# Two units of a pair of heads begin together: one visit of TensorE per pair in an attention that runs inside an MLP

## The chip, the cores and the metric

One NeuronCore of one Trainium2 chip runs the whole program. The metric is the device time of one execution in microseconds, lower is better. The engines have short names here: PE is TensorE (matmuls; PEld its weight loads), ACT is ScalarE, DVE is VectorE, POOL is GpSimd, SP is SyncE, which issues nearly all DMAs.

## The reference

Windowed causal attention with a linear bias (window 128, 8 batches, 8 heads, 576 positions, 64 features per head), and then an MLP with the Mish activation on its output (4608 tokens, 512 to 2048 to 512), in float32:

```python
scores = scale * q @ k.T                      # scale = 1/8
bias = -slope[h] * |i - j|
scores = where(0 <= i - j < 128, scores + bias, -1e9)
attn = softmax(scores)
x = (attn @ v), heads side by side            # 4608 x 512
h = x @ w_in
g = h * tanh(softplus(h))                     # Mish
out = g @ w_out
```

## The kernel before, in words

**Work of the MLP.** The tokens are taken in nine groups: the first 512 positions of each of the 8 batches, and a ninth group of the 64 positions that each batch has left. For each group `c` there are two phases on PE. In the first, `first(c, j)` for j = 0..7 makes 256 of the hidden features each, into one of two PSUM tiles with the tag `s`; `mish` on ACT brings them to SBUF. In the output phase, 32 calls of `second` (8 values of j, two halves of the tokens, two tiles `t`) make the output, six matmuls of 512 columns each into `po`. A call of `second` is called an output step here, and the 32 of a group have positions 0 to 31. Both matmuls work in float32r on split operands (a rounded part and the rest), with three products for one. The split of `g` is made by `parts(c, half, j)`, four steps ahead of its use: a copy on ACT (tile `gg`, three buffers) and a subtraction on POOL.

**Work of the attention.** The attention of batch c + 1 runs inside the output phase of group c, spread between the output steps; that of batch 0 runs ahead of everything. A batch has four pairs of heads, `p` = 0..3. A pair has a first unit (`unit(b, p, 0)`, query blocks 0 and 1), a second unit (`unit(b, p, 1)`, blocks 2 and 3) and a last unit (`last_unit`, the 64 positions left, of both heads). The steps of a unit are:

- `scores`: four products on PE into a tile `s` of two PSUM banks (tag `s`, two buffers, shared with `first`). The last unit writes its scores into a free part of the first unit's tile.
- `exps(0)`, `exps(1)`: for each block and head one DVE operation (add the bias, take the minimum) and one exponential with its sum on ACT, into `pz`.
- `fold`: POOL adds the two halves of the window into one square; DVE makes reciprocals of the sums. `scale`: DVE multiplies by these.
- `weights`: four transposes on PE into the same `s` tile, then one DVE product with the two triangular masks, which spreads the square again.
- `values`: products with `v` on PE into the tile `o`, one PSUM buffer for a pair; the first unit begins it, the second ends it. `split_x` (second unit only): copy on ACT, subtraction on DVE, which give the operand `x` of the MLP.

The last unit has the same steps in small; its `fold` ends with a copy on ACT, and its `values` with a DVE copy and a DMA to `xs`.

**What sets the order.** Every engine call goes through `InOrder`, which keeps each engine's instructions in the order in which the program makes them. The order is that of a sorted list of steps, each with a time. `attention(b)` gives the steps of a batch, with one unit of time per unit of heads: unit `k = 2 p + half` starts at time k. In the output phase these times are put on the scale of output steps, `(n - 2) / 9.0 * s - 0.2` with n = 32, so that a unit of time is 3.33 output steps. Entries of `parts` stand at 2 m - 4.1 for the m-th of 16. In the output phase of group 0 four late conversions of weights (`converting`) are in the list too, at fixed positions from 0.3 to 10.1; each takes ACT, DVE and POOL.

`load_pair` and `load_v` issue the loads of the pair after next (two buffers each).

The one place where times differ between first and second unit is the end of `unit`: all units have the same list, and the products with values of unit k, at k + 1.99, come just ahead of the scores of unit k + 2.

Of the kernel before, what the change touches and what calls it, by code (L numbers as in the profile page):

```python
# [35 lines left out]
def attention_mish_mlp(  # L36
# [70 lines left out]
    def load(dst, src):  # L107
        sp.dma_start(out=dst, in_=src)

    def load_w(kind, j):  # L110

        n = 256 if kind == "i" else DM
        if kind == "i":
            src = w_in[:, j * 256 : (j + 1) * 256].rearrange("(c p) f -> p c f", p=P)
        else:
            src = w_out[j * 256 : (j + 1) * 256, :].rearrange("(c p) f -> p c f", p=P)
        if (kind, j) == last_w:

            halves = [
                xp.tile([P, 1024], U32, tag=f"x{NCC - 2 + a}", name=f"w{kind}{j}_{a}")  # L120
                for a in range(2)
            ]
        else:
            t = big(f"w{kind}{j}", U32)
            halves = [t[:, :1024], t[:, 1024:]]
            whole[(kind, j)] = t
        raw_w[(kind, j)] = halves
        for a, t in enumerate(halves):
            part = src[:, a * (512 // n) : (a + 1) * (512 // n), :]
            if bits:  # L130
                load(t.rearrange("p (c n) -> p c n", n=2 * n), part.bitcast(U32))
            else:
                load(t[:, :512].bitcast(F32).rearrange("p (c n) -> p c n", n=n), part)
# [122 lines left out]
    def load_pair(b, p):  # L256
        hs = slice(2 * p, 2 * p + 2)
        qk = at.tile([P, 2, S], F32, tag="qk", name=f"qk{b}_{p}")
        load(qk[:, 0, :], qT[b, hs].rearrange("h d s -> (h d) s"))
        load(qk[:, 1, :], kT[b, hs].rearrange("h d s -> (h d) s"))  # L260
        z = qd[p % 2]
        for i in range(2):
            r = slice(i * D, (i + 1) * D)
            load(z[r, r], qT[b, 2 * p + i, :, CH:S])
        qkv[(b, p)] = (qk, z)

    def load_v(b, p):
        cs = slice(p * P, (p + 1) * P)
        va = at.tile([P, 4, P], F32, tag="va", name=f"va{b}_{p}")
        load(va, v[b, 0:CH, cs].rearrange("(k p) d -> p k d", p=P))  # L270
        load(vb[p % 2][:64], v[b, CH:S, cs])
        qkv[("v", b, p)] = (va, vb[p % 2])
# [3 lines left out]
    def unit(b, p, half):  # L276
# [23 lines left out]
        def exps(a):  # L300
            if a == 0:
                st["mx"] = at.tile([P, 4], F32, tag="mx", name=f"mx{name}")
                st["sm"] = at.tile([P, 4], F32, tag="sm", name=f"sm{name}")
                st["pz"] = at.tile([P, 4, 256], F32, tag="pz", name=f"pz{name}")
            mx, sm, pz = st["mx"], st["sm"], st["pz"]
            n = 256 if blocks[a] else P
            for i in range(2):
                c = 2 * i + a

                dve.tensor_tensor_reduce(  # L310
                    out=pz[:, c, :n], in0=st["s"][:, i, 256 * (a + 1) - n : 256 * (a + 1)],
                    in1=nb[:, 2 * p + i, 256 - n :], scale=-SCALE, scalar=3.0e38,
                    op0=ALU.add, op1=ALU.min, accum_out=mx[:, c : c + 1],
                )
                act.activation(
                    pz[:, c, :n], pz[:, c, :n], AF.Exp, bias=mx[:, c : c + 1], scale=-1.0,
                    accum_out=sm[:, c : c + 1],
                )
# [48 lines left out]
        def split_x():  # L367
            if half == 1:
# [4 lines left out]
                    out=x[:, 1, :], in0=o, in1=x[:, 0, :].bitcast(F32), op=ALU.subtract  # L373
                )

        return [
            (0, scores), (0.02, lambda: exps(0)), (0.25, lambda: exps(1)), (0.7, fold), (0.95, scale),
            (1.3, weights), (1.99, values), (2.02, split_x),
        ]

    def last_unit(b, p):
# [61 lines left out]
    def attention(b):  # L443

        steps = []
        for k in range(2 * NP):
            p, half = divmod(k, 2)  # L450
            for u in [unit(b, p, half)] + ([last_unit(b, p)] if half == 0 else []):
                steps += [(k + d, f) for d, f in u]
            if half:
                nxt = (b, p + 2) if p + 2 < NP else (b + 1, p + 2 - NP)
                if 0 < nxt[0] < B:
                    steps.append((k + 0.03, lambda nxt=nxt: load_pair(*nxt)))
                    steps.append((k + 2.01, lambda nxt=nxt: load_v(*nxt)))
        return sorted(steps, key=lambda s: s[0])

    def last_x():  # L460
# [14 lines left out]
    def first(c, j, blocks=range(NCC)):  # L475
        if blocks[0] == 0:
            hs[j % 2] = ps.tile([P, 2, CH], F32, tag="s", name=f"h{c}_{j}", bufs=2)
        h = hs[j % 2]
        for t, cc in (
            [(t, cc) for cc in blocks for t in range(2)] if len(blocks) < NCC  # L480
            else [(t, cc) for t in range(2) for cc in blocks]
        ):
            x = xt[(c, cc)]
            for k, (w_, x_) in enumerate(((0, 0), (0, 1), (1, 0))):
                pe.matmul(
                    h[:, t, :], lhsT=w_part("i", j, w_, cc)[:, t * P : (t + 1) * P],
                    rhs=x[:, x_, :], start=(cc == 0 and k == 0), stop=(cc == NCC - 1 and k == 2),
                )
# [3 lines left out]
    def mish(c, j):  # L492
        if j % 2 == 0:
            gt[(c, j // 2)] = big(f"g{c}_{j // 2}", F32).rearrange("p (f n) -> p f n", n=CH)
        f = 2 * (j % 2)
        act.activation(gt[(c, j // 2)][:, f : f + 2, :], hs[j % 2], AF.Mish)
# [3 lines left out]
    def parts(c, half, j):  # L500

        src = gt[(c, j // 2)][:, 2 * (j % 2) : 2 * (j % 2) + 2, half * 256 : (half + 1) * 256]
        gg = ff.tile([P, 2, 2, 256], F32R, tag="gg", name=f"gg{c}_{half}_{j}", bufs=3)
        gh, gl = gg[:, 0], gg[:, 1]
        act.activation(gh, src, AF.Copy)
        pool.tensor_tensor(out=gl, in0=src, in1=gh.bitcast(F32), op=ALU.subtract)
        gs[(c, half, j)] = (gh, gl)
# [53 lines left out]
    def run(steps):  # L561
        for _, work in sorted(steps, key=lambda s: s[0]):
            work()

    def converting(weights, times, sign):

        steps = []
        for (kind, j), at_ in zip(weights, times):
            st = []
            steps.append((at_[0], lambda kind=kind, j=j, st=st: st.extend(convert_w(kind, j, sign))))  # L570
            steps += [(t, lambda n=n, st=st: st[n]()) for n, t in enumerate(at_)]
        return steps
# [12 lines left out]
    def stages(*times):  # L585
        t, d, u, low = times
        return t, t + 0.01, d, d + 0.01, u, low

    early = attention(0) + converting(
        conv[:3],  # L590
        [stages(4.3, 4.85, 5.6, 5.7), stages(5.5, 6.4, 7.1, 7.2), stages(7.0, 8.1, 8.7, 8.8)], True,
# [11 lines left out]
    for c in range(B + 1):  # L603

        steps = []
        for j in range(NJ):
            if c or j:
                steps.append((j, lambda j=j: first(c, j)))
            steps.append((j + 0.9, lambda j=j: mish(c, j)))
        steps += [(NJ - 1.05, lambda j=j: parts(c, 0, j)) for j in range(2)]  # L610
        if c == 0:
            starts = [-0.5 + 0.84 * n for n in range(9)]
            steps += converting(
                conv[3:12], [(t, t + 0.42, t + 0.3, t + 0.72, t + 1.15, t + 1.2) for t in starts], False
            )
        run(steps)
        if c == 0:
            load_w(*last_w)

        n = 4 * NJ  # L620
        steps = []
        for m in range(2 * NJ):
            for t in range(2):
                steps.append((2 * m + t, lambda m=m, t=t: second(c, *divmod(m, NJ), t)))
            if m >= 2:
                steps.append((2 * m - 4.1, lambda m=m: parts(c, *divmod(m, NJ))))
        if c == 0:
            steps += converting(
                conv[12:],
                [  # L630
                    stages(0.3, 1.2, 2.8, 2.9), stages(2.0, 3.0, 4.8, 4.9),
                    stages(4.0, 5.0, 6.8, 6.9), stages(7.0, 8.0, 10.0, 10.1),
                ],
                True,
            )
        if c + 1 < B:
            steps += [((n - 2) / 9.0 * s - 0.2, f) for s, f in attention(c + 1)]
        elif c + 1 == B:
            steps.append((4.5, last_x))
        run(steps)  # L640
# [63 lines left out]
```

## Time and profile before

| | |
|---|---|
| median of 3 runs | 1049.19 us (1048.67 to 1049.48) |
| the profiled execution | 1048.58 us, of which the span is 1046.9 us |
| PE busy | 1005.4 us (96% of the span) |
| ACT, DVE, POOL busy | 402.1, 345.6, 315.8 us |
| mean granted clock of PE | 0.984 |
| output phase with the attention of batch 1 (112.5 to 198.5 us) | 86.0 us, clock 0.92 |
| output phase with the attention of batch 2 (243.9 to 309.0 us) | 65.1 us, clock 1.00 |

The span runs from the first to the last instruction of the program; the execution's own time is 1.7 us longer. In the timeline views a row starts with the time from the span's start and the time to the end of the last instruction of the row, and like instructions in a row are merged with their count; a bracket names the idle time of the engine ahead of the row and what ended it. Float32 products appear twice in the counts. The tile names are the program's: `h<-x,si` is `first`, `po<-so,gg` is `second`, `s<-qk` the scores, `s<-qk,qd` the scores of the last unit, `s<-ident,pz` the transposes, `o<-pz,va` the products with values, `pt_` and `pz_` with a number and an l the tiles of the last unit.

### The profile page before, as it was taken

To read this page: it belongs to the slowest core of one execution; us is meant where nothing else is said; L and a number is where in the kernel's file an instruction comes from. 1 tells how busy PE (TensorE), PEld (TensorE's weight loads), DVE (VectorE), ACT (ScalarE), POOL (GpSimd) and SP (SyncE) were. 2 spreads that over 40 slices of the span, in tenths; PEclk is the share of its full clock that TensorE was granted. 3 is DMA by queue.
4 is the path that set the end of the run, shared out by engine and by line. 5 is a ranking of instruction groups with operands and counts; after the bars stand their busy time and mean duration, and the time that the engine had idled before them with its cause. 6 is when DMAs were issued, how large, how long until landed. Compare 5 with 4: busy or idle time off the path is not lost.

```text
span 1046.9 us, 14298 instructions
## 1 busy us (share of the span) xinstructions
PE 1005.4 (96%) x5394; PEld 792.9 (76%) x5394; DVE 345.6 (33%) x1084; ACT 402.1 (38%) x945; POOL 315.8 (30%) x287
## 2 busy tenths in 40 slices
PE   7669869999999999999999999999999999999998
PEld 5458647787778777887788777877787778888886
DVE  5669555303540255005610553035402550010000
ACT  4547745215431444234512542154314442231121
POOL 2445765203430243014400342034302430141042
PEclk9979989999999999999999999999999999999999
DMA  8950112200320022002210122002200101010001
GB/s 274 398 176 1 65 36 59 68 1 26 92 70 1 23 61 74 32 1 62 92 34 0 41 79 69 1 26 94 70 1 24 60 14 41 1 41 21 1 1 41
DMA packets 52133, 59.33 MB, mean 57 GB/s; under 512 B 13024, under 2 KB 32608, under 8 KB 52064
## 3 DMA queue, kind: packets, MB, share of 16 engines
q1 hardware_dynamic: 50880, 57.69, 17.1%
q8 instruction: 43, 0.70, 0.3%
q10 hardware_dynamic: 1184, 0.72, 0.2%
q14 instruction: 26, 0.21, 0.1%
HBM read 47.91 MB, written 10.49 MB: 56 GB/s over the span
## 4 chain that ended last, share of the span: by engine, by line
PE 88%; POOL 3%; issue 1%; ACT 1%; DVE 1%; POOLq 0%
PE h L30 38%; PE po L30 36%; PE s L30 8%; PE o L30 5%; POOL wo L30 1%; POOL so L30 1%; DVE pz L30 1%; DVE to L30 1%; POOL pz L30 0%; ACT to L30 0%; POOL gg L30 0%; ACT so L30 0%; PE pt_3l L30 0%; ACT pz L30 0%; PE pt_2l L30 0%
## 5 line engine op out<-in xcount | busy, mean ns | idle before, releaser
L30 PE MATMUL po<-so,gg 128*128 128x512 f32 x1728 | 434.0, 402 | 0.0
L30 PE MATMUL h<-x,si 128*128 128x512 f32 x1728 | 394.6, 390 | 0.0
L30 POOL TENSOR_TENSOR gg<-g,gg 128x512 fp32r<-128x512 f32 x144 | 185.3, 1290 | 649.9 <-ACT gg L30 547.2
L30 PEld LDWEIGHTS h<-x,si 128*128 128x128 f32 x1728 | 324.9, 188 | 67.8 <-ACT g L30 0.2
L30 PEld LDWEIGHTS po<-so,gg 128*128 128x128 f32 x1728 | 317.8, 190 | 74.0 <-issue 5.5
L30 DVE CUSTOM_DVE_ANT_0 pz<-s,nb 128x256 f32<-128x256 f32 (+1 forms) x256 | 84.4, 386 | 305.6 <-PE s L30 295.9
L30 ACT ACTIVATE g<-h 128x1024 f32<-128x1024 f32 x72 | 73.9, 1027 | 270.0 <-PE h L30 270.0
L30 ACT ACTIVATE pz<-pz,mx 128x256 f32<-128x256 f32 (+1 forms) x256 | 120.5, 472 | 135.3 <-DVE mx L30 135.3
L30 ACT ACTIVATE gg<-g 128x512 fp32r<-128x512 f32 x144 | 88.5, 622 | 44.8 <-PE po L30 43.3
L30 DVE TENSOR_TENSOR pz<-s,masks 128x1024 f32<-128x1024 f32 x64 | 78.2, 1222 | 21.4 <-PE s L30 21.3
L30 DVE TENSOR_TENSOR pz<-pz,s 128x512 f32<-128x512 f32 x64 | 43.9, 685 | 104.3 <-POOL pz L30 104.3
L30 POOL TENSOR_TENSOR pz<-pz 128x256 f32<-128x256 f32 x64 | 64.4, 1007 | 26.0 <-ACT pz L30 18.1
L30 PE MATMUL s<-ident,pz 128*128 128x128 f32 x256 | 40.1, 280 | 21.2 <-DVE pz L30 11.4
L30 PE MATMUL s<-qk 64*128 64x128 f32 (+1 forms) x448 | 57.7, 376 | 0.0
L30 PEld LDWEIGHTS s<-ident,pz 128*128 128x128 f32 x256 | 31.8, 143 | 31.0 <-issue 12.1
L30 PE MATMUL o<-pz,va 128*64 128x128 f32 (+1 forms) x560 | 54.9, 325 | 0.1
L30 PEld LDWEIGHTS o<-pz,va 128*64 128x64 f32 x560 | 33.3, 136 | 28.1 <-issue 13.1
L30 DVE COPY ob<-po 128x512 f32<-128x512 f32 x18 | 12.5, 692 | 117.3 <-PE po L30 117.3
L30 ACT ACTIVATION_READ_ACCUMULATOR pz<-pz,mx 128x1 f32 x256 | 48.0, 187 | 0.0
L30 PEld LDWEIGHTS s<-qk 64*128 64x128 f32 x448 | 33.9, 186 | 11.2 <-issue 8.2
L30 DVE TENSOR_TENSOR x<-o,x 128x512 fp32r<-128x512 f32 x32 | 22.1, 692 | 58.0 <-ACT x L30 58.0
L30 ACT ACTIVATE x<-o 128x512 fp32r<-128x512 f32 x32 | 18.8, 587 | 53.8 <-PE o L30 53.4
(121 smaller groups left out, 475.8 us busy)
## 6 DMA issues: line engine op xcount, KB each, us to landing
wi<-in_moe_w_in_dram SPq DMA_DIRECT2D x16, 512.0 KB, 10.6
wo<-in_moe_w_out_dram SPq DMA_DIRECT2D x16, 512.0 KB, 10.3
out_dram<-ob SPq DMA_DIRECT2D x32, 256.0 KB, 2.0
qk<-in_q_dram SPq DMA_DIRECT2D x28, 288.0 KB, 3.6
qk<-in_k_dram SPq DMA_DIRECT2D x28, 288.0 KB, 3.8
va<-in_v_dram SPq DMA_DIRECT2D x28, 256.0 KB, 2.8
first<-in_q_dram SPq DMA_DIRECT2D x4, 288.0 KB, 3.6
first<-in_k_dram SPq DMA_DIRECT2D x4, 288.0 KB, 4.2
```

What stands on the lines that cost most here:

```text
L30: return self.tc.keep_in_program_order(method(*args, **kwargs))
```

## The change

From the second batch on, the second unit of a pair has a list of its own: it begins at the same time as the first unit, does its steps behind those of the first, and its products with values come right behind the first unit's, ahead of the next pair's scores. A pair so spans two units of time and a little, the batch 8 units in place of 9, and a unit of time becomes 30 / 8 = 3.75 output steps. The load of `v` comes one unit of time earlier. For all other units (batch 0, and the first units) `values` moves from 1.99 to 1.98 in the list.

```diff
@@ unit
+        if b and half == 1:
+            return [
+                (-0.995, scores), (-0.5, lambda: exps(0)), (-0.25, lambda: exps(1)), (0.2, fold),
+                (0.45, scale), (0.75, weights), (0.99, values), (1.02, split_x),
+            ]
         return [
             (0, scores), (0.02, lambda: exps(0)), (0.25, lambda: exps(1)), (0.7, fold), (0.95, scale),
-            (1.3, weights), (1.99, values), (2.02, split_x),
+            (1.3, weights), (1.98, values), (2.02, split_x),
         ]
@@ attention
                     steps.append((k + 0.03, lambda nxt=nxt: load_pair(*nxt)))
-                    steps.append((k + 2.01, lambda nxt=nxt: load_v(*nxt)))
+                    steps.append((k + (1.03 if b else 2.01), lambda nxt=nxt: load_v(*nxt)))
@@ output phase of group c
         if c + 1 < B:
-            steps += [((n - 2) / 9.0 * s - 0.2, f) for s, f in attention(c + 1)]
+            steps += [((n - 2) / 8.0 * s - 0.2, f) for s, f in attention(c + 1)]
```

## The prediction

> **What bounds the kernel now.** I read the page's span and its list of DMA issues (last column: us to landing) and the engine times by stretch; then the timelines of PE, ACT, DVE and POOL inside one batch.
>
> ```profile
> span 1046.9 us, 14298 instructions
> ...
> va<-in_v_dram SPq DMA_DIRECT2D x28, 256.0 KB, 2.8
> ```
>
> ```profile
> 112.50:198.50 86.00, 72.61 (x414) 53.88 (x414) 44.30 (x135) 45.39 (x112) 48.85 (x37) 0.92 0.19 60
> 243.90:309.00 65.10, 65.10 (x410) 49.65 (x410) 35.02 (x124) 31.66 (x97) 26.77 (x26) 1.00 0.21 63
> ```
>
> Columns of the second fence: stretch, length, busy time of PE, PEld, DVE, ACT, POOL, granted clock, DMA share, GB/s. They are the output phases of the first two batches that carry the attention of the next batch. The second (243.9 to 309.0, batch 2) is the steady form: PE busy 65.10 of 65.10 us at clock 1.00. There the time is the sum of PE's own work, so any new wait of PE is lost outright. Batch 1 has 13.4 us in which PE is idle, at clock 0.92, because late weight conversions share ACT, DVE and POOL with the attention.
>
> PE inside batch 2 (columns: start, time to the last end, instruction, count):
>
> ```profile
> 221.62 22.38 PE L30 MATMUL h<-x,si 128*128 128x512 f32 x98
> ...
> 243.93 0.93 PE L30 MATMUL s<-qk 64*128 64x128 f32 x8
> ...
> 245.25 5.72 PE L30 MATMUL po<-so,gg 128*128 128x512 f32 x24
> 250.90 1.13 PE L30 MATMUL s<-qk 64*128 64x256 f32 x8
> 251.97 1.66 PE L30 MATMUL po<-so,gg 128*128 128x512 f32 x6
> 253.46 0.60 PE L30 MATMUL s<-ident,pz 128*128 128x128 f32 x4
> 253.90 0.27 PE L30 MATMUL pt_0l<-ident,pz_0l 128*128 128x128 f32 x1
> 253.92 3.00 PE L30 MATMUL po<-so,gg 128*128 128x512 f32 x12
> 256.85 0.87 PE L30 MATMUL o<-pz,va 128*64 128x256 f32 x8
> ...
> 258.74 0.69 PE L30 MATMUL s<-qk,qd 128*128 128x96 f32 x4
> 259.21 1.63 PE L30 MATMUL po<-so,gg 128*128 128x512 f32 x6
> 260.68 0.60 PE L30 MATMUL s<-ident,pz 128*128 128x128 f32 x4
> 261.03 3.00 PE L30 MATMUL po<-so,gg 128*128 128x512 f32 x12
> 263.96 1.09 PE L30 MATMUL o<-pz,va 128*64 128x128 f32 x12
> ...
> 266.04 1.66 PE L30 MATMUL po<-so,gg 128*128 128x512 f32 x6
> ...
> 307.66 1.09 PE L30 MATMUL o<-pz,va 128*64 128x128 f32 x12
> 308.68 0.50 PE L30 MATMUL po<-so,gg 128*128 128x512 f32 x1
> ```
>
> A plain matmul of 512 columns costs (243.93 - 221.62) / 98 = 0.228 us; an output step of six costs 1.36. The 24 between two visits took 5.65 us instead of 5.45, so a visit costs 0.2 around itself as well. Visit lengths, first row to next `po`: scores of the second unit alone 250.90 to 251.97, 1.07; values and scores of a second unit 263.96 to 266.04, 2.08; values of the last second unit 307.66 to 308.68, 1.02.
>
> **What the change removes.** Per batch ten visits become five: each visit of a second unit is joined to the one of the first unit. What stays of the joined work is its bare streaming. Four transposes of 128 columns started 253.46 to 253.90, 0.11 each; by that rate the scores of a second unit (4 x 256 columns) cost 0.88, its values (1024 columns) 0.88. Saved: first visit 1.07 + 0.2 - 0.88 = 0.4; each of three middle visits 2.08 + 0.2 - 1.76 = 0.52, together 1.56; last visit 1.02 + 0.2 - 0.88 = 0.34. Sum 2.3 us a batch. Transposes stay as many; their stops cost no switch (0.35 us for four, 260.68 to 261.03).
>
> Of this the Trainium skill says, in "TensorEngine Tiling (Array Packing)", Key Properties, that changing the tiling mode drains the array, while changing the tile does not. By that rule a middle join removes three of seven mode changes; at half of 0.34 each that is 0.51, and the trace agrees with 0.52. [...]
>
> **What it adds: waits.** The second unit loses the slack it had. Steps are now 3.75 positions per unit, and from the start of a pair's first output step (call it P) five steps run to the transposes of the first unit: 5 x 1.36 + 0.1 = 6.9 us, as in `weights` at 1.3. In pairs 0 and 2 one step then separates these from the last block's transpose and another from the second unit's (`weights` at 0.75); in pairs 1 and 3, by rounding, first unit and last block share a stop and only one step follows. The rows for the chain:
>
> ```profile
> 244.03 1.02 ACT L30 ACTIVATE g<-h 128x1024 f32<-128x1024 f32 x1 [3.31 <-PE h L30]
> ...
> 246.37 0.40 ACT L30 ACTIVATE pz<-pz,mx 128x128 f32<-128x128 f32 x1
> ...
> 247.16 0.61 ACT L30 ACTIVATE gg<-g 128x512 fp32r<-128x512 f32 x1
> 247.68 0.50 ACT L30 ACTIVATE pz<-pz,mx 128x256 f32<-128x256 f32 x1
> ...
> 248.66 0.44 ACT L30 ACTIVATE pz_0l<-pz_0l,mx_0l 128x192 f32<-128x192 f32 x1
> ...
> 249.10 0.62 ACT L30 ACTIVATE gg<-g 128x512 fp32r<-128x512 f32 x1
> 252.07 0.40 ACT L30 ACTIVATE pz_0l<-pz_0l,sm_0l 128x128 f32<-128x128 f32 x1 [2.35 <-POOL pz_0l L30]
> ...
> 259.80 0.40 ACT L30 ACTIVATE pz<-pz,mx 128x128 f32<-128x128 f32 x1 [3.57 <-DVE mx L30]
> ```
>
> ```profile
> 249.80 1.28 POOL L30 TENSOR_TENSOR gg<-g,gg 128x512 fp32r<-128x512 f32 x1 [0.60 <-ACT gg L30]
> 251.04 0.72 POOL L30 TENSOR_TENSOR pz<-pz 128x256 f32<-128x256 f32 x1
> 251.72 0.32 POOL L30 TENSOR_TENSOR pz_0l<-pz_0l 128x64 f32<-128x64 f32 x1
> ...
> 255.86 1.30 POOL L30 TENSOR_TENSOR pz<-pz 128x512 f32<-128x512 f32 x1
> ```
>
> ```profile
> 251.79 0.69 DVE L30 TENSOR_TENSOR pz<-pz,s 128x512 f32<-128x512 f32 x1 [2.14 <-POOL pz L30]
> 254.09 1.23 DVE L30 TENSOR_TENSOR pz<-s,masks 128x1024 f32<-128x1024 f32 x1 [0.24 <-PE s L30]
> 255.24 0.41 DVE L30 TENSOR_TENSOR pf_0l<-pt_0l,masks 128x256 f32<-128x256 f32 x1
> 259.46 0.29 DVE L30 CUSTOM_DVE_ANT_0 pz<-s,nb 128x128 f32<-128x128 f32 x1 [1.24 <-PE s L30]
> ```
>
> At the start of a batch: `s` has two PSUM buffers; the second unit's is the one of the last `first`, which Mish reads until 245.05. Its scores would start at 243.93 + about 0.76, so PE waits 0.4.
>
> First unit's transposes, pairs 0 and 1: DVE starts at 259.46, when the last-block scores (258.74 + 0.69) have ended, 0.25 after P; ACT at P + 0.59. ACT then does, in its order: two narrow exps 0.79, one `gg` 0.52, two wide exps 0.98, last block 0.44, and now, ahead of the next `gg`, two wide exps of the second unit, another 0.98: `gg` from 4.3 to 4.92. POOL subtracts from 5.0 and begins `fold` 1.24 later, at 6.24; DVE's `scale` starts 0.75 after that and takes 0.69: 7.7. PE wanted it at 6.9: 0.8 in each. In pairs 2 and 3 `fold` comes ahead of that `gg` and nothing is late.
>
> Second unit's transposes, pairs 1 and 3: its `scale` is queued on DVE behind the two mask products, and the first of these waits for the first unit's transposes. From these: 0.63 (253.46 to 254.09) + 1.15 + 0.41 + 0.69 = 2.9. PE has 0.46 of transposes and a step of 1.36 + 0.1, 1.9. Wait 0.9 or so in each.
>
> The same, pair 0: two steps lie between, enough for that queue; but POOL's fold of the second unit is behind another `gg`, which is behind ACT's copy of the last block (POOL's last fold from 6.92 to 7.25, copy to 7.65, `gg` to 8.25, its subtraction to 9.55, fold to 10.85, scale to 11.55). PE is there at 7.7 + 0.35 + 1.45 + 0.1 + 1.4 = 11.0. Wait 0.55. In pair 2, where PE was not held before, 0.1 to 0.2. Behind each of these waits stand only output steps; their `gg` tiles were made four steps ahead, so ACT and POOL gain time and nobody else is late.
>
> Values of the second unit follow their transposes by one step and the first unit's values, 0.35 + 1.45 + 0.7 = 2.5, against 0.63 + 1.23 for the mask product: hidden, with 0.6 to spare. If that cover went, each 0.1 of lateness would cost 2.8 us over 28 pairs.
>
> DMA: the `v` load moves from 3.01 to 2.04 after its pair began. The buffer it takes is free by then, it lands in 2.8 us and is used more than a pair (some 16 us, 243.93 to 259.21) later; on SP's queue only output and `xs` writes stand behind it. Nothing; without that cover PE would wait 2.8 at the values. The edit of 1.99 to 1.98 passes no other entry: nothing.
>
> New waits: 0.4 + 0.8 + 0.8 + 0.9 + 0.9 + 0.55 + 0.15 = 4.5 us; minus 2.3: +2.2 a batch, six steady batches +13.
>
> **Batch 1** is the unknown.
>
> ```profile
> 125.37 0.66 PE L30 MATMUL s<-ident,pz 128*128 128x128 f32 x4 [3.10 <-DVE pz L30]
> ...
> 142.20 1.08 PE L30 MATMUL s<-ident,pz 128*128 128x128 f32 x4 [7.21 <-DVE xo_0l L30]
> ...
> 154.13 1.09 PE L30 MATMUL s<-ident,pz 128*128 128x128 f32 x4 [2.57 <-DVE pz L30]
> ```
>
> PE waits 12.9 us in these three. `scale` of the first unit now sorts behind the second conversion's bit work on DVE (3.36 against 3.0; it was 2.97), so the first wait grows; the second unit's folds come earlier, so the 7.2 shrinks. The same conversions, folds and subtractions pass POOL up to the end of pair 1, and they set the end there, so I take 0. Ends: all three waits go, -12.9; they double, +12.9.
>
> Sum: 1048.58 (the profiled execution: span 1046.9 and 1.7 around it) + 13 = 1061.6; the median of the runs is 0.6 above that execution: 1062.
>
> **Rivals.** (a) *The gain stays* (0.12): DVE and POOL do not hold the work in the order of its positions; second `scale` passes the mask products, folds pass the `gg` subtractions, and only the 0.4 at the start is lost: 7 x (2.3 - 0.4) = 13 won, 1036. For it: no wait of PE in batch 2 now. Against: the DVE rows (`scale`, then mask product, then last block) have the order of the positions. It decides once the waits of a batch stay under 2.3. (b) *The first unit's DVE work starts at its own scores' end* rather than after the last block's (0.12): some 1.4 us earlier, so both 0.8 waits and the 0.55 go: 2.3 - 2.3 = 0 a batch, 1049 to 1051. Against: the 259.46 row follows the last-block scores. (c) *Batch 1 gets worse* (0.14): the conversions hold `scale` of pairs 0 and 1, waits double, the clock drops again; 1062 + 13 = 1075. (d) *Batch 1 gets better* (0.06): 1049.
>
> The Trainium skill, "TensorE: Matmul & The Clock Gate", The HAM clock gate, has the clock halve after an idle window of about 3.4 us. By that the steady waits, under 1 us each, cost no clock, and those of (c) do; the 0.92 beside waits of 3 to 7 us agrees.
>
> **How the numbers follow.** Forecast 0.56, its own range 1055 to 1069 (each wait 0.2 either way, batch 1 within 4). The range 1047 to 1075 leaves out (a) and a part of (c) and (d). A measurement tells 0.2% (2 us) from no change: faster 0.12 and a part of (d), 0.15; same 0.07 from (b) and (d); slower 0.78.
>
> **What would show it.** In batch 2 of the new profile: five visits of PE, the middle ones near 4.1 us; PE rows of transposes with waits on DVE `pz` of 0.8 to 0.9 in pairs 0, 1 and 3, none at values; a wait on ACT `g` of 0.4 at each batch start; the phase 67.3 instead of 65.1. Wrong if PE is busy throughout that phase, if the waits sit at the values, or if batch 1 moves by more than the six others together.

## The result, and the profile after

The changed kernel takes 1079.33 us (median of 5 runs, 1078.34 to 1080.92), the kernel before 1049.19 (1048.34 to 1049.56): a ratio of 1.029, 95% interval 1.028 to 1.030. It is slower, as forecast, but by 30 us where the prediction had 13, and outside its range.

The engine times by stretch, after: output phase of the first batch, one steady phase (batch 2), another steady phase (batch 4), and a piece of the latter. The columns are those of the two stretches of before; these here run to the end of the output phase, while those of before ended some 2 us sooner, with output steps still to come, so lengths are compared in the table below.

```profile
112.40:202.70 90.30, 73.89 (x421) 56.44 (x421) 45.49 (x136) 45.51 (x112) 48.91 (x37) 0.89 0.19 59
246.30:317.80 71.50, 66.68 (x421) 51.85 (x421) 36.47 (x126) 31.63 (x97) 26.75 (x26) 1.00 0.20 60
476.50:549.00 72.50, 68.07 (x421) 53.03 (x421) 36.38 (x126) 31.62 (x97) 26.79 (x26) 0.98 0.20 59
488.90:492.30 3.40, 3.40 (x10) 2.62 (x10) 1.74 (x3) 0.63 (x1) 2.51 (x2) 0.50 0.00 0
```

PE, which was busy for all of a steady phase, now has nearly 5 us of idle time in it. In some phases there is also a stretch of 3.4 us at half the clock (last row). From the PE timelines I took the length of each phase, from a batch's first scores to the first matmul of the next `first`:

| | batch 1 | batches 2 to 7, each |
|---|---|---|
| before | 87.75 | 67.62 (all six) |
| after | 90.25 | 71.5 (2 and 3), 72.5 (4 to 7) |
| difference | +2.5 | 2 x 3.9 + 4 x 4.9 = +27.4 |

Together that is 29.9 us, against 29.7 between the spans (1046.9 and 1076.6). The timeline of PE in batch 2, after; a bracket is idle time, counted from the modelled end of the matmul ahead, so that starts show some 0.2 us more:

```profile
246.32 0.93 PE L30 MATMUL s<-qk 64*128 64x128 f32 x8
247.50 1.13 PE L30 MATMUL s<-qk 64*128 64x256 f32 x8 [0.26 <-ACT g L30]
248.56 0.69 PE L30 MATMUL s<-qk,qd 128*128 128x96 f32 x4
249.03 7.09 PE L30 MATMUL po<-so,gg 128*128 128x512 f32 x30
258.10 0.66 PE L30 MATMUL s<-ident,pz 128*128 128x128 f32 x4 [1.98 <-DVE pz L30]
...
259.99 0.27 PE L30 MATMUL pt_0l<-ident,pz_0l 128*128 128x128 f32 x1
...
262.02 0.66 PE L30 MATMUL s<-ident,pz 128*128 128x128 f32 x4 [0.37 <-DVE pz L30]
...
263.99 1.74 PE L30 MATMUL o<-pz,va 128*64 128x256 f32 x20
...
268.08 7.08 PE L30 MATMUL po<-so,gg 128*128 128x512 f32 x30
275.91 0.66 PE L30 MATMUL s<-ident,pz 128*128 128x128 f32 x4 [0.74 <-DVE pz L30]
...
278.80 0.66 PE L30 MATMUL s<-ident,pz 128*128 128x128 f32 x4 [0.74 <-DVE pz L30]
```

The joined visit is there: 263.99 to 268.08, 4.09 us, where the two of before took 2.36 and 2.08 and another 0.2 around the second. So are the waits: Mish at the start (0.26), first transposes of pairs 0 and 1 (1.98, 0.74), second ones (0.37, 0.74). The one that is out of size is the first of a batch. ACT of the same stretch shows why:

```profile
246.42 1.02 ACT L30 ACTIVATE g<-h 128x1024 f32<-128x1024 f32 x1 [3.32 <-PE h L30]
249.66 1.28 ACT L30 ACT_TABLE_LOAD   x1 [2.22 <-DVE mx L30]
250.96 0.40 ACT L30 ACTIVATE pz<-pz,mx 128x128 f32<-128x128 f32 x1
...
251.75 0.61 ACT L30 ACTIVATE gg<-g 128x512 fp32r<-128x512 f32 x1
...
254.68 0.61 ACT L30 ACTIVATE gg<-g 128x512 fp32r<-128x512 f32 x1
```

Before, the table load (Mish and the exponential use different tables) ran while PE and DVE were at the scores. Now ACT stands idle for 2.22 us until DVE's first result, and the load only then starts: 1.28 us more ahead of the first exponential. The programs differ at this place (table load, first exponential, and what each waits for):

```
before  ACT_TABLE_LOAD
        ACTIVATE pz <- pz, mx   [waits DVE]
after   ACT_TABLE_LOAD          [waits DVE]
        ACTIVATE pz <- pz, mx   [waits POOL]
```

With a second wait, the one for DVE had been put ahead of the load. The trace shows it: a semaphore instruction of ACT that waits for DVE ends at 249.62, and the load begins at 249.66; so it is in all six steady batches. The Trainium skill, "ScalarE: Activation LUTs", What ACT_TABLE_LOAD costs, gives 1283 ns for a load; the 1.28 of the rows agrees.

### The profile page after: what moved, and what is told of

Read it like the earlier page. It is cut to its first block, busy times and chain, and to the rows that moved or that the text cites. A ratio compares the mean times of both kernels' runs of the same rounds, so it can differ in the third digit from the quotient of the medians.

```text
span 1076.6 us, 14292 instructions
## 1 busy us (share of the span) xinstructions
PE 1004.9 (93%) x5394; PEld 800.2 (74%) x5394; DVE 345.9 (32%) x1084; ACT 399.5 (37%) x945; POOL 315.8 (29%) x287
## 4 chain that ended last, share of the span: by engine, by line
PE 76%; ACT 7%; POOL 5%; issue 4%; DVE 3%; POOLq 0%; DVEq 0%; ACTq 0%
PE h L30 37%; PE po L30 26%; PE s L30 8%; PE o L30 4%; ACT pz L30 3%; DVE pz L30 2%; POOL gg L30 2%; ACT gg L30 1%; POOL pz L30 1%; POOL so L30 1%; POOL wo L30 1%; ACT L30 1%; ACT g L30 1%; ACT pz_0l L30 0%; ACT to L30 0%
## 5 line engine op out<-in xcount | busy, mean ns | idle before, releaser
L30 PEld LDWEIGHTS po<-so,gg 128*128 128x128 f32 x1728 | 324.6, 193 | 65.5 <-issue 0.8
L30 PE MATMUL s<-ident,pz 128*128 128x128 f32 x256 | 42.4, 290 | 46.7 <-DVE pz L30 44.1
L30 PEld LDWEIGHTS s<-ident,pz 128*128 128x128 f32 x256 | 29.5, 144 | 65.1 <-DVE pz L30 53.6
L30 PE MATMUL s<-qk 64*128 64x128 f32 (+1 forms) x448 | 52.0, 366 | 1.8 <-ACT g L30 1.8
L30 PE MATMUL o<-pz,va 128*64 128x128 f32 (+1 forms) x560 | 49.7, 325 | 0.0
```

The costliest lines, as they stand in the source:

```text
L30: return self.tc.keep_in_program_order(method(*args, **kwargs))
```

## The experiments

Times of before beside them are 1048.9 to 1049.3 us, each taken on the same chip. A "phase" is that of the table above.

**The table load.** From batch 2 on, one exponential of one column at the start of a batch. It stands in the list right behind the first unit's scores, and is ACT's first work of the batch:

```diff
+            if c:
+                steps.append((-0.19, lambda: act.activation(warm[:, 1:], warm[:, :1], AF.Exp)))
```

> The changed kernel, and from batch 2 on one exponential of a single column on ACT ahead of a batch's first scores, so that the table load (1.28 us) doesn't stand behind ACT's wait for DVE. Theory (the late table load holds the first transposes of a batch 1.3 us more, and the 2 us wait that results halves the clock in four of six batches, 1.0 us each): PE's wait ahead of the first transposes falls from 2.1 to 0.8 us, no half-clock stretch is left behind batch 1, and the time falls by 6 x 1.3 + 4 x 1.0 = 12, to 1067. Rival (the exponentials themselves are late, through DVE or the PSUM buffer that Mish reads): the table load moves, the wait stays at 2.1, 1079.

Measured: 1067.11 us, ratio 1.017 (1.016 to 1.019). ACT and PE in batch 2 of this kernel:

```profile
247.77 1.28 ACT L30 ACT_TABLE_LOAD   x1
249.06 0.20 ACT L30 ACTIVATE warm<-warm 128x1 f32<-128x1 f32 x1
249.99 0.40 ACT L30 ACTIVATE pz<-pz,mx 128x128 f32<-128x128 f32 x1 [0.72 <-DVE mx L30]
```

```profile
257.17 0.66 PE L30 MATMUL s<-ident,pz 128*128 128x128 f32 x4 [0.74 <-DVE pz L30]
```

The wait falls to 0.74, all six steady phases are 70.3, and no half-clock stretch is left behind batch 1. The load gives 6 x 1.2 = 7.3 us, the clock 4 x 1.0 = 4.1: together 11.4 of the 12.2 measured, where the theory asked for 12.

**What the clock did.** In the changed kernel the same wait of 1.98 us comes in every steady batch, and the clock fell in four of six. In the two kernels of the last experiment below, whose steady batches are the same code, it fell in all six. PE in batch 4, after:

```profile
488.33 0.66 PE L30 MATMUL s<-ident,pz 128*128 128x128 f32 x4 [1.98 <-DVE pz L30]
488.75 2.79 PE L30 MATMUL po<-so,gg 128*128 128x512 f32 x6
```

An output step takes 2.6 us here where it takes 1.47 in batch 2. Whether a wait of 2 us costs this hangs on where it falls in time. In each of the traces all changes of the granted clock lie on one grid of 3.413 us (in the changed kernel 20 changes, all within 0.001 us of it). These are windows of that grid, around the waits of batches 2 (two windows), 3 and 4; PE's idle time is the length less the busy time that follows it:

```profile
253.36:256.78 3.42, 2.77 (x13) 1.95 (x11) 1.27 (x8) 2.92 (x11) 1.84 (x3) 1.00 0.00 0
256.78:260.19 3.41, 2.09 (x12) 1.78 (x13) 2.18 (x4) 0.92 (x3) 2.31 (x4) 1.00 0.00 0
369.42:372.83 3.41, 1.83 (x9) 1.18 (x7) 0.73 (x5) 2.04 (x8) 2.24 (x3) 1.00 0.00 0
485.46:488.88 3.42, 1.44 (x9) 0.94 (x9) 0.96 (x3) 1.96 (x7) 2.24 (x3) 1.00 0.01 2
```

The wait of batch 2 is split into 0.65 and 1.32 us, that of batch 3 leaves 1.58 us in its fuller window, and neither costs the clock; that of batch 4 lies whole in one window, and the next one is the row at 0.50 above. Over all traces of this case, from 70 to 1030 us of the span, each window at full clock with 1.90 us of idle PE or less was followed by full clock, and each with 1.97 us or more (58 of them) by half; none lay between. The idle time counts from the modelled ends of matmuls. That may also be why the runs of the changed kernel spread by 2.6 us and those of before by 1.2; the mean clock was 0.978 in its shortest run and 0.970 in its two longest, but how many batches fell in each is not on record, so this is not shown.

**Which scores DVE waits for.** The last unit's scores ahead of the second unit's:

```diff
-                (-0.995, scores), ...
+                (-0.985, scores), ...
```

> The changed kernel with the last unit's scores ahead of the second unit's. Theory (DVE's first operation of a pair waits for the last unit's scores, as they write the same tile; and the second unit's wait for Mish is covered by them): DVE starts 0.9 us earlier in each pair, the first transposes of pair 1 don't wait (0.9 less), those of pair 0 wait 1.3 in place of 2.1, too short for the clock to drop, and the 0.4 at a batch's start goes: 6 x 2.1 + 4 x 1.0 = 17 less, 1062, batch 1 left aside. Rival (DVE waits for the first unit's own scores alone, the transposes are held by something else): only the 0.4 goes, 1077.

Measured: 1068.80 us, ratio 1.019 (1.017 to 1.020); phases 70.3, clock full. The wait at the start and the first one of pair 1 are gone, that of pair 0 is 0.96 by starts (0.80 in its row; 1.3 was expected), so the theory holds: DVE's first operation does wait for the last unit's scores. But the gain is 10.5 and not 17. Batch 1 lost 1.3, and a pair's visit grew from 4.09 to 4.44 us. The PE rows of that visit:

```profile
266.78 0.93 PE L30 MATMUL s<-qk 64*128 64x128 f32 x8
267.64 0.69 PE L30 MATMUL s<-qk,qd 128*128 128x96 f32 x4
268.25 1.14 PE L30 MATMUL s<-qk 64*128 64x256 f32 x8
269.32 0.97 PE L30 MATMUL po<-so,gg 128*128 128x512 f32 x3
```

The last unit's scores use the whole array (128 rows, `128*128` in its row), the others half of it (`64*128`). Standing between two sets of half-array products they cost 0.35 us more, at four of the five visits of a batch; I put that down to two changes more between half and whole array.

**The queue of the second unit's scale.** Ahead of the first unit's mask product:

```diff
-                (0.45, scale), (0.75, weights), ...
+                (0.25, scale), (0.75, weights), ...
```

> The changed kernel with the second unit's scale on DVE ahead of the mask products of the first unit (time 0.25 in place of 0.45). Theory (the second transposes of pairs 1 and 3 wait since scale is queued behind the mask product, which waits for the first transposes): in pair 1 the fold is ready by 8.5 us after the pair's first step, scale by 9.2, and the wait of 0.9 goes; in pair 3 the fold itself stands on POOL behind a subtraction and ends at 8.9, so 0.8 stays, now through POOL. 7 x 0.9 = 6 less, 1073. Rival (POOL's fold holds both): no change, 1079.

Measured: 1074.78 us, ratio 1.025 (1.023 to 1.026). In pair 1 the second transposes don't wait any more, in pair 3 they still do, 0.74 us: both as expected. Steady phases fell by 0.95, batch 1 grew by 2.2 (92.5), since there the mask product is now late and the values wait 1.77 us for it.

**Batch 1 in the old order:**

```diff
-        if b and half == 1:
+        if b > 1 and half == 1:
```

and the old scale of 9 for it.

> The changed kernel with batch 1 in the old order and the old scale, so that its output phase is the one of the kernel before. Theory (batch 1 costs 2.5 us of the 30, through waits beside the conversions): 1077, the phase 87.8 us in place of 90.3. Rival (the order in batch 1 also sets buffers and clock windows of the batches behind it): the phases of batches 2 to 7 change too.

Measured: 1073.57 us, ratio 1.024 (1.022 to 1.025). The first phase is back at 87.8, so batch 1 costs the 2.5. The rest comes from the batches behind it, as the rival had it: batch 2 has a phase of 70.2 (its first exponential follows a batch in the old order and its table load is early), and the clock fell in three batches in place of four.

**The second unit's fold and scale.** The wait for POOL that holds the table load should be for the second unit's fold in pair 3, which the change had put behind POOL's last `gg` subtraction:

```diff
-                ... (0.2, fold), (0.45, scale), ...
+                ... (-0.045, fold), (0.25, scale), ...
```

> The changed kernel with the second unit's fold at -0.045 (ahead of the last subtraction of POOL in a batch) and its scale at 0.25 (ahead of the mask products); no added exponential. Theory (the table load stands behind ACT's wait for DVE only since the first exponential of a batch waits for POOL as well, and that is for the last fold, which had become POOL's last work of the attention): the table load is early again, the first transposes of a batch wait 0.9 in place of 2.1, no clock drop; and the second transposes of pairs 1 and 3 don't wait (0.9 each), nor those of pair 0 (0.55). Steady phase 71.5 - 1.25 - 1.8 - 0.5 = 67.9 us, the time 1067 - 6 x 2.35 = 1053, batch 1 up to 2 more as with the early scale alone. Rival (the wait for POOL is for something else of POOL): table load late, 2.1 us stay, clock drops: phase 69.2 to 70.2, 1063.

Measured: 1050.46 us, ratio 1.0016 (1.0007 to 1.0025), steady phases 67.6. In its trace the first exponential waits for DVE alone and the load is early, without any added work. The time is 3 us under the expected 1053. ACT of this kernel, and PE in pairs 0 and 1:

```profile
246.36 1.28 ACT L30 ACT_TABLE_LOAD   x1
248.52 0.40 ACT L30 ACTIVATE pz<-pz,mx 128x128 f32<-128x128 f32 x1 [0.88 <-DVE mx L30]
```

```profile
255.69 0.66 PE L30 MATMUL s<-ident,pz 128*128 128x128 f32 x4 [0.68 <-DVE pz L30]
...
259.07 0.60 PE L30 MATMUL s<-ident,pz 128*128 128x128 f32 x4
...
272.85 0.66 PE L30 MATMUL s<-ident,pz 128*128 128x128 f32 x4 [0.66 <-DVE pz L30]
...
274.85 0.60 PE L30 MATMUL s<-ident,pz 128*128 128x128 f32 x4
```

Two numbers in the list undo all but 2 us of the loss. What is left is in batch 1 (89.1 against 87.75); in the steady phases the waits that stay (at the start, and ahead of the first transposes) take just what the joined visits save.

**The first unit's fold** ahead of the subtraction that it followed on POOL, on top of the early table load:

```diff
-            ... (0.7, fold), (0.95, scale),
+            ... (0.48 if b > 1 else 0.7, fold), (0.701, sums), (0.95, scale),
```

(`sums` is the part of `fold` on DVE, left where it was.)

> The kernel with the early table load, and from batch 2 on POOL's fold of the first unit ahead of the gg subtraction that it followed (0.48 in place of 0.7). Theory (the first transposes of pairs 0 and 1 wait since this fold stands behind a subtraction, whose gg copy is behind the second unit's exponentials on ACT): both waits of 0.9 go, the second unit's wait in pair 0 grows by about 0.2, the others stay. Phase 70.3 - 1.6 = 68.7, the time 1067 - 6 x 1.6 = 1057. Rival (the exponentials alone are late): no change, 1067.

Measured: 1057.45 us, ratio 1.008 (1.007 to 1.010), phases 68.7: both waits gone, the sizes as expected.

**All of it together,** with all batches and with batch 1 left in the old order. The lists of the two units:

```diff
+  first:  (0, scores), (0.02, exps 0), (0.22, exps 1), (0.28, fold), (0.78, sums), (0.8, scale), (1.1, weights), ...
+  second: (-0.995 if p else -0.985, scores), (-0.5, exps 0), (-0.25, exps 1), (-0.05, fold), (0.14, sums), (0.15, scale), (0.75, weights), ...
+  last:   weights at 1.3 in place of 1.4
```

> All waits taken away by order: folds ahead of the subtractions, the first unit's exponentials and transposes earlier (1.1), the last block's transposes at 1.3, the second unit's scale ahead of the last block's mask product, and in the first pair the last block's scores ahead of the second unit's. Theory (a joined visit saves 2.3 us a batch, and the waits were all from the order of the queues): PE has no wait in the steady phases but up to 0.2 at the start, phase 67.6 - 2.3 + 0.2 = 65.5, 6 x 2.1 = 12.6 less than the kernel before; batch 1 2 to 3 more than before: 1039. Rival (the second unit's chain doesn't fit into a pair in any order): waits of 0.5 and more come up at other transposes or at the values, phase over 67, 1049 or more.

> The same from batch 2 on, batch 1 in the old order. Theory (batch 1 loses its 2 to 3 us through the conversions alone): 1049 - 12.6 = 1036.5, the first phase 87.8 and the others 65.5. Rival (batch 1 gains as well once the folds are early): slower than the kernel with all batches in the new order.

Measured: 1048.45 us (ratio 0.9998, 0.9989 to 1.0007) and 1045.37 (0.9972, 0.9963 to 0.9981). Steady phases are 67.06 and not 65.5, the size that the rival had (a phase over 67): in pair 2 the transpose of the last block waited 1.4 us by starts for ACT's copy, which waited for POOL's last fold behind a subtraction.

```profile
290.54 0.33 PE L30 MATMUL pt_2l<-ident,pz_2l 128*128 128x128 f32 x1 [1.25 <-ACT pz_2l L30]
```

Batch 1 takes 91.7 us in the new order and 87.8 in the old. Whether the chain fits into a pair in some order, as the theory had it, was left to one more edit, with batch 1 in the old order:

```diff
-            ... (0.9, fold), (1.3 if b >= 2 else 1.4, weights)
+            ... (0.81 if b >= 2 else 0.9, fold), (1.3 if b >= 2 else 1.4, weights)
```

> The kernel with all waits reordered from batch 2 on, and the last block's fold at 0.81 in place of 0.9, so that in pair 2 it comes ahead of a gg subtraction on POOL. Theory (the one wait that was left, 1.4 us ahead of the last block's transpose in pair 2, is this queue; all that the joined visits save then shows): phase 67.06 - 1.4 = 65.65 us, 6 x 1.4 = 8.4 less than with 0.9, 1037. Rival (the wait only moves to the second unit's transposes or the values of pair 2): phase 66.5 or more, 1042 and above.

Measured: 1038.18 us, ratio 0.990 (0.988 to 0.992), against 1049.12: 11 us less than the kernel before, and the wait in pair 2 is gone. Its steady phase, by engine and by PE's first rows:

```profile
243.40:309.30 65.90, 65.88 (x421) 52.29 (x421) 36.74 (x126) 31.52 (x97) 26.87 (x26) 1.00 0.22 65
```

```profile
246.00 5.74 PE L30 MATMUL po<-so,gg 128*128 128x512 f32 x24
251.57 0.60 PE L30 MATMUL s<-ident,pz 128*128 128x128 f32 x4
...
262.29 5.73 PE L30 MATMUL po<-so,gg 128*128 128x512 f32 x24
267.86 0.60 PE L30 MATMUL s<-ident,pz 128*128 128x128 f32 x4
```

PE is busy throughout again, at full clock, and the phase is 65.84 against 67.62. Add to these 1.8 us the 0.37 that the first visit pays for its order and 0.24 of small waits in pair 2, and the joined visits save 2.4 us in a batch.

**Batch 1.** In the changed kernel PE waits there as follows:

```profile
128.57 1.11 PE L30 MATMUL s<-ident,pz 128*128 128x128 f32 x4 [6.30 <-DVE pz L30]
...
133.94 0.47 PE L30 MATMUL pt_0l<-ident,pz_0l 128*128 128x128 f32 x1 [1.69 <-ACT pz_0l L30]
...
139.53 0.66 PE L30 MATMUL s<-ident,pz 128*128 128x128 f32 x4 [2.56 <-DVE pz L30]
...
157.46 0.85 PE L30 MATMUL s<-ident,pz 128*128 128x128 f32 x4 [3.18 <-DVE pz L30]
159.95 0.47 PE L30 MATMUL pt_1l<-ident,pz_1l 128*128 128x128 f32 x1 [1.64 <-ACT pz_1l L30]
```

The prediction said that the first of these grows since the first unit's scale is behind the second conversion on DVE, and that the conversions set the end all the same. The three waits that it named add up to 12.0 us, where they had 12.9; new are the waits of the last block's transposes for ACT, 1.69 and 1.64 us, where before had 0.36 and none. A first edit moved only that scale:

```diff
-            ... (0.95, scale),
+            ... (0.84 if b == 1 else 0.95, scale),
```

> The changed kernel with the first unit's scale in batch 1 at 0.84, ahead of the second conversion's bit work on DVE (0.69 + 1.23 us) as in the kernel before. Theory (the conversions, not this place in DVE's queue, set when the first two pairs of batch 1 end): PE's first wait of 6.3 us there falls by about 1.9, the waits behind it grow by about as much, the phase stays within 1 us of 90.2 and the time at 1079. Rival (the place in DVE's queue costs what it holds up): the phase falls by 1.5 to 2.5 us, to the 87.8 of before, and the time to 1077.

Measured: 1081.61 us, ratio 1.031 (1.029 to 1.032), first phase 91.3. It told nothing on the question: the scale ran earlier, but the transposes also wait for DVE's reciprocal of the last block, which lies in the same PSUM tile and was still behind the bit work. With the last block's fold moved too:

```diff
-            (0.01, scores), (0.5, exps), (0.9, fold), ...
+            (0.01, scores), (0.5, exps), (0.845 if b == 1 else 0.9, fold), ...
```

> As the kernel with the first unit's scale of batch 1 at 0.84, and the last block's fold of batch 1 at 0.845: its reciprocal lies in the same PSUM tile as the transposes, and held them in that kernel behind the second conversion's bit work. Theory (the conversions set when the first pairs of batch 1 end): PE's first wait of 6.3 us falls by about 2, later waits grow, the phase of batch 1 stays within 1 us of 90.2. Rival (DVE's queue costs what it holds up): the phase falls to 88 or less. The other phases stay at 71.5 or 72.5 each, as the clock falls.

Measured: 1081.74 us, ratio 1.031 (1.029 to 1.032), first phase 91.3; the steady phases 72.5, all six with a fall of the clock. PE in batch 1 of this kernel:

```profile
127.52 1.11 PE L30 MATMUL s<-ident,pz 128*128 128x128 f32 x4 [4.83 <-DVE sm_0l L30]
...
132.35 0.33 PE L30 MATMUL pt_0l<-ident,pz_0l 128*128 128x128 f32 x1 [1.32 <-ACT pz_0l L30]
...
139.51 1.12 PE L30 MATMUL s<-ident,pz 128*128 128x128 f32 x4 [5.44 <-DVE pz L30]
...
158.55 1.12 PE L30 MATMUL s<-ident,pz 128*128 128x128 f32 x4 [3.67 <-DVE sm_1l L30]
```

Counted from the batch's first scores (112.46 in the changed kernel, 112.89 here), the first transposes start 1.5 us earlier, the second unit's 0.4 earlier, and those of pair 1 0.7 later: what is won ahead is given back, and where DVE does one piece of a conversion does not set the length. The rival is out, as the phase grew by 1.0 us instead of falling to 88, which is at the edge of what the theory allowed. That the conversions as a whole set the time of this stretch fits, but no run took them away or moved them, so it is not shown. Why the new order costs batch 1 its 2.5 us was not taken apart further. PE also runs slower there: 20.5 us of the phase are at half clock in the changed kernel and 13.7 in the kernel before, a mean of 0.89 in place of 0.92.

## Why the prediction was wrong in size

- **The bound and the saving** were right: PE alone bounds a steady phase, and the joined visits save 2.4 us a batch (2.3 predicted). One count in the working is off: by the rows two visits of before have six changes between forms of product (`128*128`, `128*64`, `64*128`) and the joined one three, not three of seven; the three that go, and the price of a change, agree with the 0.35 us for two more in the experiment on the order of the scores. Rival (a), in which the engines do not keep the order of the list, did not come true; the reordered kernel comes near its 1036 us only since its order was changed by hand.
- **The waits in the queues** were right in place and nearly in size, and none of the three signs of being wrong came up. By starts, with the early table load: start 0.53 (0.4 predicted), first transposes 0.9 and 0.9 (0.8, 0.8), second transposes of pairs 0, 1 and 3 0.54, 0.91 and 0.92 (0.55, 0.9, 0.9), pair 2 0.1 (0.15), values none. A wait also made the transposes behind it 0.06 longer. Net of the saving 2.7 a batch, 2.2 predicted: 3 us of the 17 that were missing.
- **The step that failed** is "First unit's transposes, pairs 0 and 1": "ACT at P + 0.59" held for pair 1 but not for pair 0, where the first exponential came at P + 1.93 (249.03 to 250.96), as the table load was behind the wait. The 0.59 was read from pair 1 of the kernel before (259.80 against 259.21), where no load stands, and taken for both pairs; the load of 1.28 us at the start of a batch is in no term of the sum, as it was hidden, and what kept it hidden was not asked. 0.8 was 2.1 (1.98 in the row): 7.3 us.
- **The clock.** That "the steady waits, under 1 us each, cost no clock" followed from the wait that was mis-sized. The rule by which the prediction judged this is too mild as well: no window has to be idle as a whole, as 1.97 us of idle PE within one of 3.41 us was enough, and in four batches of six the wait of 1.98 lay whole in one. 4.1 us.
- **Batch 1**: 0 taken, 2.5 measured. The first wait grew from 3.1 to 6.3 and the 7.2 fell to 2.6, as said, and the three waits named nearly cancel (12.9 and 12.0). What the sum had no term for are the last block's waits for ACT (+3.0) and the longer time at half clock; their cause stays open.
- Rival (b) fell with the experiment on the order of the scores: DVE does wait for the last unit's scores. Of (c) and (d), (c) was nearer, with a fifth of its price.

The load, the clock, the sizes of the other waits and batch 1 make 7.3 + 4.1 + 3 + 2.5 = 17, the difference between 13 and 30.

## What to carry to other kernels

Running like work together saved what the rows said. But PE then came sooner to each result than the queues of the other engines could give it, and each place where an early subtraction, copy or product stood ahead of the urgent one became a wait of the bound engine. Order alone, with batch 1 left as it was, made the difference between 1079 and 1038 us. When steps of a list move, write down for every engine what now stands ahead of each step, and what each first operation after a table switch waits for: a second wait there can drag the load into the chain. Where the waits of PE come near 2 us within some 3.4 us, ask what the clock does too; here it went from 1.97 us of a window on.

## What was not expected of the hardware

- A table load of 1.28 us can sit behind a wait of the exponential that it is for, once this one waits for two engines (idle 2.22 us ahead of the load); with one wait, or with other work of the same table in front, the load ran at once.
- A PE wait of 1.98 us was followed by 3.4 us of half clock in four of six batches with the same code (six of six in two other kernels): all clock changes lie on a grid of 3.413 us, and a window of it with 1.97 us or more of idle PE cost the next one half its clock, one with up to 1.90 us did not.
- Four matmuls of 128 rows put between products of 64 rows made a visit 0.35 us longer (4.09 to 4.44); an estimate from this is about 0.17 us for one change between the half array and the whole.
